# In late turns, sums of values and chunk 4's scores in one group of matmuls over four banks

## The chip, the cores and the metric

The kernel runs on one core of one Trainium2 chip. The metric is the device time of one execution in microseconds (us); the median of three runs before the change is 1108.84 us, the lowest 1106.07, the highest 1110.18.

## What is computed

Attention with a block mask over 8 batches, 8 heads, 576 positions, 64 values a head; its output, laid out as 4608 tokens of 512 values, goes through two dense layers (512 by 2048 and 2048 by 512) with a gate between. All in float32.

```python
def _attn_ref(q, k, v) -> np.ndarray:
    B, H, S, D = q.shape
    block = 64
    scale = 1.0 / np.sqrt(D)
    scores = scale * np.matmul(q, k.transpose(0, 1, 3, 2))
    pos = np.arange(S)
    block_i = pos[:, None] // block
    block_j = pos[None, :] // block
    mask = block_i >= block_j
    scores = np.where(mask, scores, -1000000000.0)
    scores = scores - np.max(scores, axis=-1, keepdims=True)
    attn = np.exp(scores)
    attn = attn / (np.sum(attn, axis=-1, keepdims=True) + 1e-09)
    return np.matmul(attn, v).astype(np.float32)

def _moe_ref(x, w_in, w_out) -> np.ndarray:
    h = x @ w_in
    g = h * (1.0 / (1.0 + np.exp(-1.702 * h)))
    return (g @ w_out).astype(np.float32)
```

## The kernel before

The 64 heads are taken in 32 pairs. One turn of the outer loop does the scores of pair n and the sums of values of pair n-1, and slips steps of the dense layers between them. The first 8 turns are early turns, the other 24 (n from 8 to 31) late turns; the change touches late turns alone.

**Attention.** The 576 rows of a head's scores are cut into five chunks: chunk 0 has 64 rows, chunks 1 to 4 have 128 each, and chunk i sees 64·(2i+1) columns: 64, 192, 320, 448, 576. `score` (L314) puts the scores of both heads into banks of PSUM, one bank a head, with chunks 3 and 0 side by side in one pair of banks and chunks 2 and 1 in another; chunk 4 is 576 wide and takes two pairs, columns 0 to 255 and 256 to 575. `weigh` (L354) lets DVE read a bank, mask it and find the row's extreme (L365, one read for each head and piece), and ACT take the exponential (L372). `normalise` (L378) inverts the row sums on DVE (L382, L385) and scales, on POOL (L390) for chunks 0 to 3 and on DVE (L392) for chunk 4. `turn` (L396) transposes 32x32 blocks on DVE (L399, L404) into the buffer `tw`, and after chunk 4 sixteen DMAs on SP's queue (L411) bring the blocks of the pair to their places in `pw`. `av` (L443) multiplies them with the values: 60 matmuls whose output columns are the 576 positions, and two ACT copies to `xr` (L465, L466). `prep` (L301) transposes the next pair's q and k on DVE into the only buffer `qk` (L306), which all scores read.

**Dense layers.** A tile has 384 tokens, twelve tiles in all. A unit of the first layer is 12 matmuls into a bank `hp` (L567); ACT takes tanh (L577), DVE forms the gated product (L578, called the gate below), ACT rounds it (L586) and POOL takes the rest (L82, `gl`). A unit of the second layer is 9 matmuls into the banks `acc` (L536), of the unit before. `split` (L500) rounds the next tile's tokens on ACT (L513, `xh`) and takes the rest on DVE (L82, `xl`).

**Banks.** PSUM has eight banks: three for `acc`, two that `hp` alternates between, and three for attention (`bank`, L90). The first bank of a late group is instead the one of the two `hp` banks that is free (`lent_bank`, L97); the unit of the first layer that follows then takes the same bank as the one before. So a late group has at most four banks: both pairs of the scores 3+0 and 2+1 take the lent one and all three; chunk 4 takes the same four; the sums take one and the lent one.

**Order.** TensorE runs its matmuls in the order in which the code writes them. The table `ORDER` gives the order of a turn: in a late turn the scores `3+0/2+1`, then `V` (the sums of the pair before), then `4` (chunk 4's scores), then `L` (`prep` of the next pair); a dash is a slot in which only steps of the dense layers run, and steps run after each slot until a quota is met. A late turn has six units of the first layer, two after each of the three groups. On DVE, ACT, POOL and SP the order is set at build time by the framework's scheduler, by priorities; the gate, tanh and `split` stand under `tc.high_priority(offset=300)`. Each engine then runs its list in that order. Chunks 1 and 3 share one buffer of exponentials (L362, `e1`), so a read of chunk 1's scores follows the transposes of chunk 3.

Of the kernel before, what the change touches and what calls it, by code (L numbers as in the profile page):

```python
# [25 lines left out]
ORDER = (  # L26
# [3 lines left out]
)  # L30

START = "1+0 - B 2/3 L C - V - 4 - a - - -"
HANDOVER = "B C - 3+0/2+1 - - V - - - 4 - - L - -"


WEIGHTS_BY = ((0, 0), (8, 13), (14.5, 32))
# [4 lines left out]
def attention_moe_kernel(  # L41
# [9 lines left out]
    nc = tc.nc  # L51
    B, H, S, D = q.shape
    DM, DF = w_in.shape
    P = 128
    BLK = 64
# [7 lines left out]
    NPAIR = B * H // 2  # L63
    HP = H // 2
    NCH = 5

    sp = ctx.enter_context(tc.tile_pool(name="sp", bufs=1))
    d2 = ctx.enter_context(tc.tile_pool(name="d2", bufs=2))
# [5 lines left out]
    def early(n):  # L74

        return n < 2 * HP
# [9 lines left out]
    turns = {"n": 0, "bank": 0, "experts": False, "late": False}  # L86
# [3 lines left out]
    def bank():  # L90
        tags = ["w0", "w1", "w2"]
        if not turns["experts"]:
            tags += ["acc0", "acc1", "acc2", "h"]
        turns["bank"] += 1
        return ps.tile([P, 512], F32, tag=tags[turns["bank"] % len(tags)], name="bank")

    def lent_bank():  # L97
        gate_bank["lent"] = True
        return ps.tile([P, 512], F32, tag=gate_bank["spare"], name="bank")
# [7 lines left out]
    def mm(**kw):  # L107
        return tc.keep_in_program_order(nc.tensor.matmul(**kw))  # L108
# [19 lines left out]
    def room(tag, shape, dt, name):  # L128
        return d2.tile(shape, dt, tag=tag, name=name, bufs=1)
# [8 lines left out]
    xr = sp.tile([P, NDC, RING], F32, name="xr")  # L138


    vp = sp.tile([P, 2, NCH, D], F32, name="vp")
    nc.gpsimd.memset(vp[BLK:P, :, NCH - 1, :], 0.0)
    vx = {}

    def values(n):

        if n not in (1, 3):
            return vp
        if n not in vx:
            vx[n] = room("xl", [P, 2, NCH, D], F32, "vx")  # L150
            nc.gpsimd.memset(vx[n][BLK:P, :, NCH - 1, :], 0.0)
        return vx[n]
# [7 lines left out]
    SLOT = (None, 0, 1, 3, 6)  # L160
    turned = sp.tile([P, 8 * NS - 4, 2, 32], F32, name="turned")
    tw, pw = [
        turned[:, x : x + 4 * NS].rearrange("p (b s) h c -> p b s h c", b=4) for x in (0, 4 * NS - 4)
    ]
# [4 lines left out]
    es = []  # L169
    for i in range(NCH):  # L170
        w, o = BLK * (2 * i + 1), 2 * BLK * i * i
        es.append(flat[:, o : o + 2 * w].rearrange("p (h k) -> p h k", h=2))

    def width(i):
        return BLK * (2 * i + 1)

    def qrange(i):
        return (0, BLK) if i == 0 else (BLK * (2 * i - 1), BLK * (2 * i + 1))
# [6 lines left out]
    for g in range(NG):  # L185
# [3 lines left out]
        for fc in range(FG):  # L189
            r = (g * FG + fc) * P  # L190
# [80 lines left out]
    raw, qk = {}, {}  # L271

    def heads(n):
        b, h = divmod(n, HP)
        return [(hd, b, 2 * h + hd) for hd in range(2)]
# [17 lines left out]
    def load_v(n):  # L293
        to = values(n)
        for hd, b, h in heads(n):
            nc.sync.dma_start(
                out=to[:, hd, 0:QC], in_=v[b, h, 0 : QC * P].rearrange("(c p) d -> p c d", p=P)
            )
            nc.sync.dma_start(out=to[0:BLK, hd, QC], in_=v[b, h, QC * P : S])
# [14 lines left out]
    def score(n, banks):  # L314

        turns["late"] = not early(n)
        if n not in stats:
            mx = d2.tile([P, NCH + 1, 2], F32, tag="mx", name="mx")
            sm = d2.tile([P, NCH, 2], F32, tag="sm", name="sm")
            stats[n] = (mx, sm)  # L320
        todo = []
        taken = 0
        for chunks in banks:

            part = []
            for lo, hi in ((0, 512),) if width(chunks[0]) <= 512 else ((0, 256), (256, S)):
                ss = []
                for _ in range(2):
                    taken += 1
                    ss.append(lent_bank() if taken == 1 and turns["late"] else bank())  # L330
                c = 0
                for i in chunks:
                    a, z = qrange(i)
                    w = min(hi, width(i)) - lo
                    for hd in range(2):
                        r = slice(hd * D, hd * D + D)

                        mm(
                            out=ss[hd][:, c : c + w], lhsT=qk[n][r, 0, a : a + P],
                            rhs=qk[n][r, 1, lo : lo + w], start=True, stop=True,  # L340
                        )
                        part.append((i, hd, lo, lo + w, ss[hd][0 : z - a, c : c + w]))
                    c += w
            todo.append(sorted(part, key=lambda x: (chunks[::-1].index(x[0]), x[2])))
        for chunks, part in zip(banks, todo):
            e = {}
            for i, hd, lo, hi, s in part:
                e[i] = weigh(n, i, hd, lo, hi, s, e.get(i))
            for i in chunks[::-1]:
                normalise(n, i, e[i])  # L350
                if not early(n):
                    turn(n, i, e[i])

    def weigh(n, i, hd, lo, hi, s, e):  # L354
        mx, sm = stats[n]
        a, z = qrange(i)
        m = z - a
        w = width(i)
        if early(n):
            e = es[i]  # L360
        elif e is None:
            e = d2.tile([P, 2, w], F32, tag=f"e{i % 2}", name="e", bufs=1)  # L362
        last = i > 0 and hi == w
        mk = mask[0:m, MW - (hi - lo) : MW] if last else mask[0:m, 0 : hi - lo]
        nc.vector.tensor_tensor_reduce(  # L365
            out=e[0:m, hd, lo:hi], in0=s, in1=mk,
            op0=ALU.add, op1=ALU.min, scale=-0.125,
            scalar=3e38 if lo == 0 else mx[0:m, NCH, hd : hd + 1],
            accum_out=mx[0:m, i, hd : hd + 1] if hi == w else mx[0:m, NCH, hd : hd + 1],
        )  # L370
        if hi == w:
            nc.scalar.activation(  # L372
                out=e[0:m, hd], in_=e[0:m, hd], func=AF.Exp, scale=-1.0,
                bias=mx[0:m, i, hd : hd + 1], accum_out=sm[0:m, i, hd : hd + 1],
            )
        return e

    def normalise(n, i, e):  # L378
        _, sm = stats[n]
        m = BLK if i == 0 else P  # L380
        c = sm[0:m, i]
        nc.vector.tensor_scalar(  # L382
            out=c, in0=c, scalar1=1e-9, scalar2=2.0, op0=ALU.add, op1=ALU.mult
        )
        nc.vector.reciprocal(out=c, in_=c)  # L385
        on = SCALE_ON[phase(n)][i]
        for hd in range(2):
            x, sc = e[0:m, hd], c[:, hd : hd + 1]
            if on == "P":
                nc.gpsimd.tensor_tensor(out=x, in0=x, in1=sc.to_broadcast([m, width(i)]), op=ALU.mult)  # L390
            elif on == "D":
                nc.vector.tensor_scalar(out=x, in0=x, scalar1=sc, scalar2=None, op0=ALU.mult)  # L392
            else:
                nc.scalar.activation(out=x, in_=x, func=AF.Copy, scale=sc)
# [48 lines left out]
    def av(n):  # L443

        b, h = divmod(n, HP)
        before_av(n)
        o = bank()
        o0 = lent_bank() if turns["late"] else bank()

        todo = []  # L450
        for i in range(1, NCH):
            c = (i - 1) * P
            todo += [(o, c, P, j, pw[:, :, SLOT[i] + j]) for j in range(i)]
            todo.append((o, c + BLK, BLK, i, pw[:, 2:4, 9 + i]))
        last = len(todo) - 1
        todo.append((o0, 0, BLK, 0, pw[:, 0:2, 10]))

        for x, (bk, c, nn, j, w) in enumerate(todo):
            for hd in range(2):
                mm(  # L460
                    out=bk[hd * D : hd * D + D, c : c + nn].rearrange("d (a c) -> d a c", c=32),
                    lhsT=values(n)[:, hd, j], rhs=w[:, :, hd], start=x in (0, last + 1), stop=x >= last,
                )
        c0 = (b % 2) * S
        nc.scalar.copy(out=xr[:, h, c0 : c0 + BLK], in_=o0[:, 0:BLK])  # L465
        nc.scalar.copy(out=xr[:, h, c0 + BLK : c0 + S], in_=o)  # L466
        m = follower(n)
        if m is not None:
            load_v(m)

    def follower(n):

        m = {0: 2, 1: 3, 2: 4, 3: None}.get(n, n + 1)
        return None if m is None or m >= NPAIR else m

    def order(n):
        return {HP: START, 2 * HP: HANDOVER}.get(n, ORDER[phase(n)]).split()

# [116 lines left out]
    ends = np.cumsum([0.0] + [NFC * chunk_time(tt) for _, tt in TILES])  # L595
# [30 lines left out]
    def before_av(n):  # L626

        need = (n // HP - 1) * S
        advance(n // HP * H, lambda: done["split"] >= need)
        assert done["split"] >= need  # L630
# [49 lines left out]
```

## Time and profile before

| what | us |
|---|---|
| median of 3 runs | 1108.84 |
| the profiled execution | 1109.41 |
| its span, first to last instruction | 1107.5 |
| PE (matmuls) busy | 1070.3 (97%) |
| DVE busy | 585.0 (53%) |
| ACT busy | 498.6 (45%) |
| POOL busy | 406.4 (37%) |

The sums below are made against the profiled execution, which is 0.57 us above the median. Times in rows of the trace count from the span's start. The late turns run from about 200 to about 955 us. Matmuls overlap, so the busy time of PE tells only that it hardly waits; how long a group of matmuls takes is read from where the next group starts. An `f32` matmul shows as two rows in the trace, so that the 60 rows of one group of sums are 30 matmuls of the list of 15 pieces for two heads.

### The profile page before, as it was taken

How to read it: one execution, taken by the hardware profiler on the slowest of the kernel's cores; microseconds unless marked ns; L12 is line 12 of the kernel's file. 1: busy time of each engine (PE TensorE's matmuls, PEld its weight loads, DVE VectorE, ACT ScalarE, POOL GpSimd, SP SyncE). 2: the span in 40 equal slices, each digit the busy share in tenths (PEclk: the TensorE clock that was granted, in tenths of full speed). 3: DMA queues.
4: the chain of work that ended last, by engine and by line, in shares of the span. 5: the costliest groups of instructions: out<-in, count | busy, mean ns of one | idle time of the engine just before them, and what ended most of it. 6: DMA issues, size and time to landing. Idle time of an engine off the chain costs nothing.

```text
span 1107.5 us, 19998 instructions
## 1 busy us (share of the span) xinstructions
PE 1070.3 (97%) x6960; PEld 915.7 (83%) x6960; DVE 585.0 (53%) x1856; ACT 498.6 (45%) x1321; POOL 406.4 (37%) x509
## 2 busy tenths in 40 slices
PE   5869999899999999999999999999999999999998
PEld 3657777788888888888888888888888888899997
DVE  6786786655645645655555555645655655211211
ACT  5865776533534534534443443443444444232322
POOL 4665565323333333333333332333333333222222
PEclk8979999999999999999999999999999999999999
DMA  8634523343434433243443333344443331200000
GB/s 172 208 90 155 147 61 80 71 96 62 102 85 86 108 77 70 60 98 77 105 96 76 79 91 71 64 109 87 86 104 69 73 89 47 54 29 1 30 1 29
DMA packets 219365, 91.25 MB, mean 82 GB/s; under 512 B 197760, under 2 KB 197760, under 8 KB 219264
## 3 DMA queue, kind: packets, MB, share of 16 engines
q1 hardware_dynamic: 214528, 89.38, 34.3%
q8 instruction: 55, 0.90, 0.3%
q10 hardware_dynamic: 4736, 0.59, 0.3%
q14 instruction: 46, 0.38, 0.1%
HBM read 45.09 MB, written 9.44 MB: 49 GB/s over the span
## 4 chain that ended last, share of the span: by engine, by line
PE 87%; DVE 4%; ACT 4%; issue 2%; SPq 1%; DMA 1%; POOL 1%; POOLq 0%; ACTq 0%; DVEq 0%
PE hp L108 35%; PE acc L108 35%; PE bank L108 16%; ACT turned L372 1%; PE bank L111 1%; SPq L411 1%; DVE wm L243 1%; ACT wm L228 1%; DVE turned L365 1%; DVE wm L232 1%; DVE wm L238 1%; DVE qk L306 0%; DVE xl L82 0%; DMA raw<-in_k_dram 0%; ACT turned L425 0%
## 5 line engine op out<-in xcount | busy, mean ns | idle before, releaser
L82 POOL TENSOR_TENSOR gl<-g,gh 128x384 fp32r<-128x384 f32 x192 | 194.4, 1013 | 545.7 <-ACT gh L586 430.3
L578 DVE SCALAR_TENSOR_TENSOR g<-g,hp 128x384 f32<-128x384 f32 x192 | 106.0, 552 | 312.2 <-ACT g L577 310.8
L108 PE MATMUL hp<-xh,wih 128*128 128x384 f32 x768 | 261.1, 340 | 4.2 <-DVE g L578 3.5
L108 PE MATMUL hp<-xh,wil 128*128 128x384 f32 x768 | 258.6, 337 | 0.0
L577 ACT ACTIVATE g<-hp 128x384 f32<-128x384 f32 x192 | 94.2, 491 | 357.3 <-PE hp L108 356.0
L108 PE MATMUL hp<-xl,wih 128*128 128x384 f32 x768 | 254.8, 339 | 0.2
L108 PE MATMUL acc<-woh,gh 128*128 128x512 f32 x576 | 233.9, 406 | 0.0
L108 PE MATMUL acc<-wol,gh 128*128 128x512 f32 x576 | 227.0, 394 | 0.0
L586 ACT CAST gh<-g 128x384 fp32r<-128x384 f32 x192 | 98.5, 513 | 157.8 <-DVE g L578 157.5
L108 PE MATMUL acc<-woh,gl 128*128 128x512 f32 x576 | 168.0, 393 | 0.3 <-POOL gl L82 0.3
L108 PEld LDWEIGHTS hp<-xh,wih 128*128 128x128 f32 x768 | 144.6, 188 | 17.1 <-DVE g L578 4.4
L108 PEld LDWEIGHTS hp<-xh,wil 128*128 128x128 f32 x768 | 144.5, 188 | 7.6
L372 ACT ACTIVATE e<-e,mx 64x64 f32<-64x64 f32 (+4 forms) x240 | 132.2, 552 | 34.2 <-DVE mx L365 34.2
L390 POOL TENSOR_TENSOR e<-e,sm 64x64 f32<-64x64 f32 (+1 forms) x192 | 113.6, 612 | 87.6 <-ACT e L372 45.2
L108 PEld LDWEIGHTS hp<-xl,wih 128*128 128x128 f32 x768 | 144.0, 188 | 1.0 <-DVE xl L82 1.0
L108 PEld LDWEIGHTS acc<-woh,gh 128*128 128x128 f32 x576 | 108.2, 188 | 34.2 <-issue 10.7
L108 PE MATMUL bank<-qk 64*128 64x320 f32 (+4 forms) x768 | 121.3, 428 | 13.9 <-DVE qk L306 11.3
L108 PEld LDWEIGHTS acc<-woh,gl 128*128 128x128 f32 x576 | 107.6, 188 | 25.4 <-POOL gl L82 1.2
L365 DVE CUSTOM_DVE_ANT_0 e<-bank,mask 64x64 f32<-64x64 f32 (+4 forms) x240 | 89.7, 417 | 67.5 <-PE bank L108 64.2
L108 PEld LDWEIGHTS acc<-wol,gh 128*128 128x128 f32 x576 | 108.4, 188 | 16.8 <-issue 0.4
L399 DVE STREAM_TRANSPOSE turned<-e 128x384 f32<-128x384 f32 (+1 forms) x192 | 92.5, 500 | 50.1 <-POOL e L390 48.4
L108 PEld LDWEIGHTS bank<-qk 64*128 64x128 f32 x768 | 69.8, 194 | 53.1 <-issue 22.1
(50 smaller groups left out, 962.3 us busy)
## 6 DMA issues: line engine op xcount, KB each, us to landing
turned<-turned SPq DMA_DIRECT2D x192, 80.0 KB, 2.1
turned<-turned SPq DMA_DIRECT2D x96, 112.0 KB, 2.2
raw<-in_q_dram SPq DMA_DIRECT2D x128, 72.0 KB, 2.3
out_dram<-osb SPq DMA_DIRECT2D x36, 256.0 KB, 2.4
raw<-in_k_dram SPq DMA_DIRECT2D x120, 72.0 KB, 2.4
turned<-turned SPq DMA_DIRECT2D x96, 88.0 KB, 2.1
words<-in_moe_w_in_dram SPq DMA_DIRECT2D x16, 512.0 KB, 6.0
vp<-in_v_dram SPq DMA_DIRECT2D x60, 128.0 KB, 2.4
```

The source lines that it names most:

```text
L82: eng.tensor_tensor(out=out, in0=in0, in1=in1, op=ALU.subtract)
L108: return tc.keep_in_program_order(nc.tensor.matmul(**kw))
L111: return tc.keep_in_program_order(nc.tensor.transpose(**kw))
L228: nc.scalar.activation(out=bits[j][:, c], in_=f(w[..., 1]), func=AF.Copy, scale=2.0**-112)
L232: nc.vector.tensor_scalar(out=u, in0=u, scalar1=3, scalar2=None, op0=ALU.logical_shift_left)
L365: nc.vector.tensor_tensor_reduce(out=e[0:m, hd, lo:hi], in0=s, in1=mk, op0=ALU.add, op1=ALU.min, scale=-0.125, scalar=3e38 if lo == 0 else ...
L372: nc.scalar.activation(out=e[0:m, hd], in_=e[0:m, hd], func=AF.Exp, scale=-1.0, bias=mx[0:m, i, hd : hd + 1], accum_out=sm[0:m, i, hd : hd ...
L390: nc.gpsimd.tensor_tensor(out=x, in0=x, in1=sc.to_broadcast([m, width(i)]), op=ALU.mult)
L399: nc.vector.transpose(out=tw[:, :, SLOT[i] : SLOT[i] + i, hd].rearrange("p b j c -> p j b c"), in_=e[:, hd, 0 : i * P],)
L577: nc.scalar.activation(out=g, in_=hp[:, 0:tt], func=AF.Tanh, scale=1.702)
L578: nc.vector.scalar_tensor_tensor(out=g, in0=g, scalar=1.0, in1=hp[:, 0:tt], op0=ALU.add, op1=ALU.mult)
L586: nc.scalar.copy(out=gh, in_=g)
```

## The change

In late turns `V` moves three slots later and the `4` of the table goes: `av` of pair n-1 now writes chunk 4's scores of pair n right behind the sums, in one group over four banks. The sums fill columns 0 to 319 of a first bank (positions 0 to 319) and 0 to 255 of a second (positions 320 to 575). Chunk 4's first 384 columns go to a bank of their own for each head, the lent one and the third; the other 192 go beside the sums, head 0's in the first bank and head 1's in the second. The copies to `xr` are 320 and 256 columns wide in place of 64 and 512. What follows the matmuls (`weigh`, `normalise`, `turn`) is unchanged and was put into a function `settle`. Early turns keep their banks and sizes.

```diff
     "1+0 - B - 2 - C - 3 L V - a - 4 -",
-    "3+0/2+1 - - - V - - 4 - - - L -",
+    "3+0/2+1 - - - - - - V - - - L -",
 )
-HANDOVER = "B C - 3+0/2+1 - - V - - - 4 - - L - -"
+HANDOVER = "B C - 3+0/2+1 - - - - - - V - - L - -"
...
         b, h = divmod(n, HP)
         before_av(n)
-        o = bank()
-        o0 = lent_bank() if turns["late"] else bank()
+        if turns["late"]:
+            o0, o = bank(), bank()
+            cut = BLK + 2 * P
+        else:
+            o, o0 = bank(), bank()
+            cut = BLK
+
+        def place(q0):
+            return (o0, q0) if q0 < cut else (o, q0 - cut)
 
         todo = []
         for i in range(1, NCH):
-            c = (i - 1) * P
-            todo += [(o, c, P, j, pw[:, :, SLOT[i] + j]) for j in range(i)]
-            todo.append((o, c + BLK, BLK, i, pw[:, 2:4, 9 + i]))
-        last = len(todo) - 1
-        todo.append((o0, 0, BLK, 0, pw[:, 0:2, 10]))
+            bk, c = place((i - 1) * P + BLK)
+            todo += [(bk, c, P, j, pw[:, :, SLOT[i] + j]) for j in range(i)]
+            todo.append((bk, c + BLK, BLK, i, pw[:, 2:4, 9 + i]))
+        todo.append((*place(0), BLK, 0, pw[:, 0:2, 10]))
...
+        m = n + 1
+        rest = []
+        if turns["late"] and m < NPAIR:
+            own = [lent_bank(), bank()]
+            a, z = qrange(4)
+            for hd in range(2):
+                r = slice(hd * D, hd * D + D)
+                mm(
+                    out=own[hd][:, 0:K4], lhsT=qk[m][r, 0, a : a + P],
+                    rhs=qk[m][r, 1, 0:K4], start=True, stop=True,
+                )
+                rest.append((4, hd, 0, K4, own[hd][0 : z - a, 0:K4]))
+            for hd, (bk, c) in enumerate(((o0, cut), (o, S - cut))):
+                r = slice(hd * D, hd * D + D)
+                mm(
+                    out=bk[:, c : c + S - K4], lhsT=qk[m][r, 0, a : a + P],
+                    rhs=qk[m][r, 1, K4:S], start=True, stop=True,
+                )
+                rest.append((4, hd, K4, S, bk[0 : z - a, c : c + S - K4]))
         c0 = (b % 2) * S
-        nc.scalar.copy(out=xr[:, h, c0 : c0 + BLK], in_=o0[:, 0:BLK])
-        nc.scalar.copy(out=xr[:, h, c0 + BLK : c0 + S], in_=o)
+        nc.scalar.copy(out=xr[:, h, c0 : c0 + cut], in_=o0[:, 0:cut])
+        nc.scalar.copy(out=xr[:, h, c0 + cut : c0 + S], in_=o[:, 0 : S - cut])
...
+        if rest:
+            settle(m, [[4]], [sorted(rest, key=lambda x: x[2])])
```

Three places in the built order follow. The new file has one line more ahead of `mm`, so its line numbers are a little higher; L369 is the read that was L365, L611 the gate that was L578, L403 and L408 the transposes L399 and L404, L307 the transpose of q and k.

**PE, the group of sums in a late turn.** Before, the last rows of the sums and what follows them (the names of counters in brackets tell which engine the row waits for):

```order
L108 MATMUL bank<-turned,vp 64x128 x6
L108 MATMUL bank<-turned,vp 64x64 x2
L108 MATMUL bank<-turned,vp 64x128 x8
L108 MATMUL bank<-turned,vp 64x64 x2
L108 MATMUL bank<-turned,vp 64x64 [waits DVE_49]
L108 MATMUL bank<-turned,vp 64x64
L108 MATMUL acc_3233<-woh,gh 128x512 [waits Activation_49]
```

Now, from the end of chunk 2's part of the sums on:

```order
L109 MATMUL bank<-turned,vp 64x64 x2
L109 MATMUL bank<-turned,vp 64x128 [waits DVE_49]
L109 MATMUL bank<-turned,vp 64x128 x5
L109 MATMUL bank<-turned,vp 64x64 x2
L109 MATMUL bank<-turned,vp 64x128 x8
L109 MATMUL bank<-turned,vp 64x64 x4
L109 MATMUL bank<-qk 128x384
L109 MATMUL bank<-qk 128x384 [waits DVE_49]
L109 MATMUL bank<-qk 128x192 x2
L109 MATMUL acc_6731<-woh,gh 128x512 [waits Activation_49]
```

The wait for DVE inside the sums stood ahead of their last two matmuls and was for the lent bank, by its counter for the gate of the unit that last used it; it now stands ahead of the first matmul into the second bank, and by its counter it is for the read of chunk 2's scores of head 0, the last to leave that bank. The scores of chunk 4 follow, and the one for head 1 waits for chunk 2's read of head 1. Four first-layer units (called h1 to h4 below) now stand between the scores 3+0 and 2+1 and the sums, in place of two; two (h5 and h6) stand between chunk 4's scores and the next turn's first scores, as before.

**DVE, from the transposes of chunk 0's and chunk 3's weights to the reads of chunks 1 and 2.** Before, the gates are those of the two units ahead of the sums:

```order
L404 STREAM_TRANSPOSE turned<-e 64x2x2x32
L578 SCALAR_TENSOR_TENSOR g<-g,hp 128x384
L404 STREAM_TRANSPOSE turned<-e 64x2x2x32
L578 SCALAR_TENSOR_TENSOR g<-g,hp 128x384
L399 STREAM_TRANSPOSE turned<-e 128x3x4x32 x2
L365 ISA e,mx<-bank,mask 128x192
L365 ISA mx 128x1
L365 ISA e,mx<-bank,mask 128x320
```

Now, in the eleventh late turn, for one:

```order
L611 SCALAR_TENSOR_TENSOR g<-g,hp 128x384
L408 STREAM_TRANSPOSE turned<-e 64x2x2x32
L611 SCALAR_TENSOR_TENSOR g<-g,hp 128x384
L408 STREAM_TRANSPOSE turned<-e 64x2x2x32
L611 SCALAR_TENSOR_TENSOR g<-g,hp 128x384 x2
L403 STREAM_TRANSPOSE turned<-e 128x3x4x32 x2
L369 ISA e,mx<-bank,mask 128x192
L369 ISA mx 128x1
L369 ISA e,mx<-bank,mask 128x320
```

Four gates, those of h1 to h4, now stand ahead of the transposes and of the reads of chunks 1 and 2; the two 128x192 rows and the two 128x320 rows that belong to the two heads are shown once. The 24 late turns fall into these kinds. In 8 turns it reads as shown: the transposes and all four reads stand behind the gate of h4. In 9 turns the transposes stand ahead of that gate and the reads (in one of these, all but the first) behind it; in 3 of these 9 a row of `xl` stands between the gate of h5 and the second transpose of the next place. In 2 turns the tile's `xh` and `xl` stand ahead of the gate of h4 and one transpose and the reads behind it. In 2 turns only the reads of chunk 2 stand behind it. In the first 3 turns all reads stand ahead of it.

**DVE, from chunk 4's reads to the next turn.** Before:

```order
L365 ISA e,mx<-bank,mask,mx 128x320
L365 ISA mx 128x1
L306 STREAM_TRANSPOSE qk<-raw 128x576 x2
L382 TENSOR_SCALAR sm<-sm 128x2
L385 RECIPROCAL sm<-sm 128x2
L392 TENSOR_SCALAR e<-e,sm 128x576 x2
L399 STREAM_TRANSPOSE turned<-e 128x4x4x32 x2
L404 STREAM_TRANSPOSE turned<-e 64x2x2x32
L578 SCALAR_TENSOR_TENSOR g<-g,hp 128x384 x2
L365 ISA e,mx<-bank,mask 64x64
```

Now:

```order
L369 ISA e,mx<-bank,mask,mx 128x192
L369 ISA mx 128x1
L307 STREAM_TRANSPOSE qk<-raw 128x576
L386 TENSOR_SCALAR sm<-sm 128x2
L389 RECIPROCAL sm<-sm 128x2
L396 TENSOR_SCALAR e<-e,sm 128x576 x2
L403 STREAM_TRANSPOSE turned<-e 128x4x4x32 x2
L408 STREAM_TRANSPOSE turned<-e 64x2x2x32
L611 SCALAR_TENSOR_TENSOR g<-g,hp 128x384
L307 STREAM_TRANSPOSE qk<-raw 128x576
L611 SCALAR_TENSOR_TENSOR g<-g,hp 128x384
L369 ISA e,mx<-bank,mask 64x64
```

One of the two transposes of q and k has moved behind chunk 4's scaling and transposes and the gate of h5; the next turn's first scores read what it writes.

More of the change, by code (lines that the diff above doesn't have):

```diff
@@ L65, in attention_moe_kernel @@
     NCH = 5
+    K4 = 384
     sp = ctx.enter_context(tc.tile_pool(name="sp", bufs=1))
@@ L344, in score, with settle @@
             todo.append(sorted(part, key=lambda x: (chunks[::-1].index(x[0]), x[2])))
+        settle(n, banks, todo)
+    def settle(n, banks, todo):
         for chunks, part in zip(banks, todo):
@@ L446, in av @@
         before_av(n)
-        o = bank()
-        o0 = lent_bank() if turns["late"] else bank()
+        if turns["late"]:
[6 more added lines that the diff above has]
+            return (o0, q0) if q0 < cut else (o, q0 - cut)
         todo = []
         for i in range(1, NCH):
-            c = (i - 1) * P
-            todo += [(o, c, P, j, pw[:, :, SLOT[i] + j]) for j in range(i)]
-            todo.append((o, c + BLK, BLK, i, pw[:, 2:4, 9 + i]))
-        last = len(todo) - 1
-        todo.append((o0, 0, BLK, 0, pw[:, 0:2, 10]))
+            bk, c = place((i - 1) * P + BLK)
+            todo += [(bk, c, P, j, pw[:, :, SLOT[i] + j]) for j in range(i)]
+            todo.append((bk, c + BLK, BLK, i, pw[:, 2:4, 9 + i]))
+        todo.append((*place(0), BLK, 0, pw[:, 0:2, 10]))
+        ends = [[x for x, y in enumerate(todo) if y[0] is bk] for bk in (o0, o)]
         for x, (bk, c, nn, j, w) in enumerate(todo):
@@ L461, in av @@
                     out=bk[hd * D : hd * D + D, c : c + nn].rearrange("d (a c) -> d a c", c=32),
-                    lhsT=values(n)[:, hd, j], rhs=w[:, :, hd], start=x in (0, last + 1), stop=x >= last,
-                )
-        c0 = (b % 2) * S
-        nc.scalar.copy(out=xr[:, h, c0 : c0 + BLK], in_=o0[:, 0:BLK])
-        nc.scalar.copy(out=xr[:, h, c0 + BLK : c0 + S], in_=o)
-        m = follower(n)
-        if m is not None:
-            load_v(m)
+                    lhsT=values(n)[:, hd, j], rhs=w[:, :, hd],
+                    start=any(x == y[0] for y in ends), stop=any(x == y[-1] for y in ends),
+                )
+        m = n + 1
[17 more added lines that the diff above has]
+                rest.append((4, hd, K4, S, bk[0 : z - a, c : c + S - K4]))
+        c0 = (b % 2) * S
+        nc.scalar.copy(out=xr[:, h, c0 : c0 + cut], in_=o0[:, 0:cut])
+        nc.scalar.copy(out=xr[:, h, c0 + cut : c0 + S], in_=o[:, 0 : S - cut])
+        nxt = follower(n)
+        if nxt is not None:
+            load_v(nxt)
+        if rest:
+            settle(m, [[4]], [sorted(rest, key=lambda x: x[2])])
     def follower(n):
```

## The prediction

> **Forecast.** Slower, 1177 us, since in 21 of the 24 late turns TensorE will stop in the middle of the sums for a bank, and then again ahead of the next scores for DVE. Both waits come from the order of DVE's list.
>
> **What bounds the kernel now.** First the page: busy times and the chain that ended last.
>
> ```profile
> PE 1070.3 (97%) x6960; PEld 915.7 (83%) x6960; DVE 585.0 (53%) x1856; ACT 498.6 (45%) x1321; POOL 406.4 (37%) x509
> PE 87%; DVE 4%; ACT 4%; issue 2%; SPq 1%; DMA 1%; POOL 1%; POOLq 0%; ACTq 0%; DVEq 0%
> ```
>
> TensorE (PE) carries 87% of the chain; DVE has half its time free. The averages mix stages, so next the busy times by stage (PE, PEld, DVE, ACT, POOL, then granted clock, DMA share, GB/s), for the late turns:
>
> ```profile
> 300.00:960.00 660.00, 658.99 (x4362) 570.01 (x4361) 361.13 (x1188) 276.95 (x744) 221.22 (x285) 1.00 0.37 82
> ```
>
> In 660 us PE is idle for 1 us, and its clock stays at 1.00. So a late turn is as long as its matmuls, and anything that makes PE wait there is paid in full. One late turn in the chain of waits (start, us, what):
>
> ```profile
> 499.44 2.04 PE bank L108 x16
> 501.48 2.24 PE acc L108 x9
> 503.72 2.10 PE hp L108 x12
> 505.82 2.08 PE acc L108 x9
> ...
> 510.02 2.92 PE bank L108 x60
> 512.93 2.26 PE acc L108 x9
> ...
> 521.49 1.17 PE bank L108 x8
> 522.66 2.27 PE acc L108 x9
> ...
> 531.22 0.57 PE bank L108
> ```
>
> The x16 group is the scores 3+0 and 2+1, x60 the sums, x8 chunk 4's scores, each followed by two second-layer and two first-layer units. From 499.44 to 531.22 the turn takes 31.78 us. A second-layer unit takes 2.08 us, but 2.24 to 2.27 just behind a group of attention: each group costs some 0.18 us at its end.
>
> **What the change gains.** Chunk 4's scores lose a group of their own: one slow unit less, 0.18 us. Their 576 columns for each head stay; at the rate of the sums (2.92 us for 1600 columns a head) they take 1.05 in place of 1.17, if the switch from sums to scores inside a group costs nothing, which no row here shows. Bounds 0 and 0.4 us a turn; I take 0.30, what the two terms give. For 24 turns: **-7.2 us**. The copies to `xr` (320 and 256 columns for 512 and 64) and the reads (384 and 192 for 256 and 320) have as many elements as before, on engines with free time. One lent bank fewer a turn saves nothing, as PE waits for no gate now (658.99 of 660).
>
> Without any wait, from the sums' start to the next turn's first scores PE would need 2.92 + 1.05 + 2.26 + 2.10 + 2.08 + 2.10 = 12.5 us.
>
> **What the change adds: the wait for a bank.** The second half of the sums goes to the bank that head 0's scores of chunks 2 and 1 leave. In the kernel before, DVE came to these reads just when the sums ran, and nobody waited, as the sums used other banks. That stretch (start, us, engine) is the model for the new order:
>
> ```profile
> 509.95 2.99 PE L108 MATMUL bank<-turned,vp 128*64 128x128 f32 x60
> 510.11 0.49 ACT L577 ACTIVATE g<-hp 128x384 f32<-128x384 f32 x1 [2.56 <-PE hp L108]
> 510.64 0.56 DVE L578 SCALAR_TENSOR_TENSOR g<-g,hp 128x384 f32<-128x384 f32 x1 [3.30 <-ACT g L577]
> 511.11 1.03 DVE L399 STREAM_TRANSPOSE turned<-e 128x384 f32<-128x384 f32 x2
> 511.23 0.51 ACT L586 CAST gh<-g 128x384 fp32r<-128x384 f32 x1 [0.62 <-DVE g L578]
> 512.28 0.36 DVE L365 CUSTOM_DVE_ANT_0 e<-bank,mask 128x192 f32<-128x192 f32 x1
> 512.57 0.35 DVE L365 CUSTOM_DVE_ANT_0 e<-bank,mask 128x192 f32<-128x192 f32 x1
> 512.68 0.46 ACT L372 ACTIVATE e<-e,mx 128x192 f32<-128x192 f32 x1 [0.95 <-DVE mx L365]
> 512.84 0.49 DVE L365 CUSTOM_DVE_ANT_0 e<-bank,mask 128x320 f32<-128x320 f32 x1
> 513.26 0.08 DVE L365 DVE_READ_ACCUMULATOR2_ANT mx<- 128x1 f32 x1
> ...
> 518.32 0.31 DVE L404 STREAM_TRANSPOSE turned<-e 64x128 f32<-64x128 f32 x1
> ```
>
> The gate of the unit ahead of the sums starts 0.69 us after them (tanh must see that unit's last matmul), then come the transposes, the reads, and head 0's read of chunk 2 is out at 513.34, 3.39 us after the sums' start. In the changed list the gate ahead is h4's, and the same rows follow. PE reaches the second half after 512 of 1600 columns, at 0.93 us.
>
> - *8 turns* with transposes and reads behind h4's gate: wait 3.39 - 0.93 = 2.46 us.
> - *9 turns* with the reads directly behind the gate: they start at 1.16 (511.11), the bank is out after steps of 0.29, 0.27, 0.42 and 0.08 at 2.22: wait 1.29.
> - *2 turns* where a tile is split there: three `xh` and three `xl` stand ahead as well.
>
> ```profile
> 540.07 2.10 ACT L513 CAST xh<-xr 128x384 fp32r<-128x384 f32 x4 [0.74 <-PE hp L108]
> 540.62 1.63 DVE L82 TENSOR_TENSOR xl<-xr,xh 128x384 fp32r<-128x384 f32 x3 [1.49 <-ACT xh L513]
> ```
>
> At 0.52 and 0.54 us each they bring the reads from 2.33 to about 3.9 and the release to 4.96: wait 4.0.
> - *2 turns* with only chunk 2's reads behind the gate: 1.16 + 0.42 + 0.08, wait 0.73.
> - *First 3 turns*: none, as all reads stand ahead.
>
> **What the change adds: the wait for q and k.** Behind this wait DVE has more to do than PE. Its list goes on through chunks 2 and 1 to 518.63 (8.68 us after the sums' start, measured above, POOL's steps included), and only then to chunk 4. For chunk 4 these rows:
>
> ```profile
> 524.25 1.44 DVE L306 STREAM_TRANSPOSE qk<-raw 128x576 f32<-128x576 f32 x2
> 524.68 0.76 ACT L372 ACTIVATE e<-e,mx 128x576 f32<-128x576 f32 x1
> 525.61 0.13 DVE L382 TENSOR_SCALAR sm<-sm 128x2 f32<-128x2 f32 x1
> ...
> 528.51 0.56 DVE L578 SCALAR_TENSOR_TENSOR g<-g,hp 128x384 f32<-128x384 f32 x1
> ```
>
> and from the groups by form (busy us, mean ns of one):
>
> ```profile
> L365 DVE CUSTOM_DVE_ANT_0 e<-bank,mask 128x448 f32<-128x448 f32 x40 | 23.1, 610 | 0.0
> L365 DVE CUSTOM_DVE_ANT_0 e<-bank,mask 128x320 f32<-128x320 f32 x40 | 17.9, 486 | 0.0
> ```
>
> A 384-wide read lies between the 320 and 448 ones, 0.55 us, 0.48 a step with the overlap of 0.07 seen above. Two of them and one of 192 columns (0.33) bring us to 9.98; the two exponentials start there and at 10.74; the row sums' step follows the second's start by 0.93 (524.68 to 525.61), 11.67; from it to the gate are 2.90 (to 528.51), 14.57. Then the gate of h5 (0.47 a step) and the second transpose of q and k (0.72), which before stood ahead of all this: 15.8 us. The next scores wait for it.
>
> PE is there at 12.5 + 2.46 = 15.0 in the 8 turns, so 15.8 decides, 3.3 us lost. In the 9 turns ACT takes the exponentials as soon as L586's copy is out (511.74, 0.94 before 512.68), and the chain ends 0.9 earlier, at 14.9 against 13.8 for PE: 2.4 lost. In 3 of these a row of `xl` stands ahead of that transpose and waits for L586 of h5 (out at 14.8) and an `xh`: 14.8 + 0.52 + 0.54 + 0.72 = 16.6, 1.75 more. In the 2 turns with chunk 2 alone behind the gate, 2.3. Of the first 3 turns two have the same late transpose, with chunk 4 some 2 us earlier but one transpose more ahead of its 192-wide reads: 13.7, 1.2 lost. The sixteen DMAs start up to 2 us later against the next scores, but the sums come two units (8.4 us) later, so their wait grows only in the last turn (under 1 us, left out).
>
> **The clock.** PE has had waits of this size in early turns:
>
> ```profile
> 202.60 0.44 PE L108 MATMUL hp<-xh,wih 128*128 128x384 f32 x1 [1.71 <-DVE g L578]
> ...
> 222.23 4.64 PE L108 MATMUL bank<-turned,vp 128*64 128x128 f32 x60 [2.50 <-DMA turned<-turned]
> ```
>
> with the stages around them:
>
> ```profile
> 200.00:205.00 5.00, 3.29 (x16) 2.81 (x17) 4.83 (x16) 1.13 (x2) 1.02 (x1) 1.00 0.00 0
> 222.00:224.00 2.00, 1.77 (x27) 1.80 (x29) 1.84 (x7) 0.40 (x2) 0.53 (x1) 0.74 0.78 126
> 224.00:226.00 2.00, 2.00 (x25) 2.00 (x23) 1.26 (x7) 1.67 (x8) 0.85 (x2) 0.50 0.96 257
> ```
>
> After 2.50 us of waiting the clock fell to 0.50 and the sums took 4.64 in place of 2.92, 1.7 us more; after 1.71 it stayed at 1.00. So waits of 1.3 cost no clock and those of 2.46 may: PE would reach the next scores at 16.7 in place of 15.8, 4.2 lost. I take 3.75, the middle, for the 8 turns; for the 2 turns with 4.0 of wait 4.0 + 1.7 = 5.7.
>
> [...]
>
> **The sum.** 8 x 3.75 + 9 x 2.4 + 3 x 1.75 + 2 x 5.7 + 2 x 2.3 + 2 x 1.2 = 30.0 + 21.6 + 5.3 + 11.4 + 4.6 + 2.4 = 75.3; less 7.2 is +68.1 on the profiled 1109.41 us. That one lies 0.57 above the median, so **1177 us**.
>
> **Rivals.**
>
> *Only the bank costs.* DVE catches up behind the sums and the clock holds: 8 x 2.46 + 9 x 1.29 + 2 x 4.0 + 2 x 0.73 = 40.8, less 7.2: 1142. For it: chunk 4's rows were put together from pieces. Against: each piece has its row, and the chain ends later than PE in every kind.
>
> *The clock holds at full rate*, and both waits stand: 71.7 less 7.2, 1173; for it the 1.71 us row, against it the 2.50 us row. [...]
>
> *Faster.* The reads of chunks 2 and 1 are out by 0.93 us after the sums' start, and DVE is never late: 1109.41 - 0.57 - 7.2 = 1102. Place: head 0's read of chunk 2; it decides from 0.93 on. For it: the first late turns stand so, and DVE has 45% of the stage free. Against: the gate that it queues behind starts at 0.69 at the earliest and lasts 0.56.
>
> *Nothing moves*, since the waits fall into time that PE loses already. PE loses 1 us in 660 there.
>
> **How the numbers follow.** Forecast 0.62, clock holds 0.20, only the bank 0.13, faster 0.03, nothing 0.02. The low end is 1142. For the high end every wait slows the clock (8 turns 4.2, six of the 9 turns 13.8 + 1.7 - 12.5 = 3.0: +7), the merge gains nothing (+7) and the chains are 0.3 us longer in 21 turns (+6): 1197. A measurement of this kernel can tell about 0.5%, 5.5 us, from no change: faster 0.03, same 0.02, slower 0.95.
>
> **What would show it.** PE idle inside `bank<-turned,vp` with DVE's `mx` as releaser, about 21 times 0.7 to 4 us; PE idle ahead of `bank<-qk` with DVE's `qk` as releaser; granted clock under 1.00 in some late slices; DVE well over 4% of the chain; a turn of 34 to 35 us. Wrong if PE's idle time in 300 to 960 us stays near 1 us: then DVE's list does not bind; if the sums wait but the scores don't, the chain of chunk 4 is too long here.

## The result, and the profile after

The changed kernel takes **1180.93 us** in the median of six runs (1177.8 to 1185.23) against 1108.93 us for the kernel before beside it (1106.07 to 1111.17): a ratio of 1.0651, with a 95% interval of 1.0633 to 1.0669. The forecast was slower, 1177 us, between 1142 and 1197. The profiled execution has a span of 1179.2 us and a mean granted clock of 0.974; before, these were 1107.5 us and 0.987.

The page of the changed kernel, busy times and the chain that ended last:

```profile
PE 1088.2 (92%) x6960; PEld 931.8 (79%) x6960; DVE 586.3 (50%) x1856; ACT 496.9 (42%) x1321; POOL 406.0 (34%) x509
PE 68%; DVE 14%; ACT 8%; issue 5%; POOL 4%; DMA 1%; DVEq 0%; POOLq 0%; SPq 0%; ACTq 0%
```

DVE does the same work as before (586.3 us against 585.0), but its share of the chain goes from 4% to 14%, and that of PE from 87% to 68%. The stage of the late turns, with the columns of before (PE, PEld, DVE, ACT, POOL, clock, DMA share, GB/s):

```profile
300.00:960.00 660.00, 609.61 (x3891) 526.03 (x3892) 333.72 (x1092) 252.33 (x683) 201.40 (x262) 0.98 0.35 77
```

PE now stands idle for 50 of 660 us where it stood idle for 1, and its clock is no longer at 1.00 throughout (0.98 in the mean). The view of waits, from 230 to 1040 us, names the two places:

```profile
PE bank L109 <- DVE mx L369: 33.9, 21, 2.4
PE bank L109 <- DVE qk L307: 23.7, 16, 3.1
```

The first is the wait for the bank inside the sums, the second the wait for q and k ahead of the next scores. One late turn in the chain of waits, from the unit ahead of the sums on; the sums start at 610.00 (start, us, what):

```profile
607.96 2.12 PE hp L109 x12
...
610.16 0.50 ACT g L610
...
611.15 1.04 DVE turned L403 x2
...
612.33 0.36 DVE e L369
...
618.78 0.56 DVE e L369
...
620.26 0.86 ACT e L376 x2
...
624.87 0.56 DVE g L611
625.42 0.70 DVE qk L307
...
626.16 2.11 PE bank L109 x16
```

Between 610.16 and 626.16 the chain does not touch PE: it runs through h4's tanh, DVE's list with the steps of ACT and POOL that it waits for, and ends with the second transpose of q and k. PE works in that stretch, but what it does is not what the next scores wait for. In the timeline, the rows of PE that end a wait (in brackets the idle time and its releaser), from most of the kinds of turn:

```profile
332.20 3.55 PE L109 MATMUL bank<-turned,vp 128*64 128x128 f32 x40 [2.34 <-DVE mx L369]
473.86 2.10 PE L109 MATMUL bank<-turned,vp 128*64 128x128 f32 x40 [1.91 <-DVE mx L369]
591.02 2.11 PE L109 MATMUL bank<-qk 64*128 64x448 f32 x16 [1.05 <-DVE qk L307]
613.44 2.10 PE L109 MATMUL bank<-turned,vp 128*64 128x128 f32 x40 [2.34 <-DVE mx L369]
626.16 2.11 PE L109 MATMUL bank<-qk 64*128 64x448 f32 x16 [0.90 <-DVE qk L307]
647.38 2.10 PE L109 MATMUL bank<-turned,vp 128*64 128x128 f32 x40 [1.16 <-DVE mx L369]
662.35 2.72 PE L109 MATMUL bank<-qk 64*128 64x448 f32 x16 [3.13 <-DVE qk L307]
```

The second half of the sums takes 2.10 us at full clock; behind the wait at 332.20 it takes 3.55, behind the equal wait at 613.44 it does not. From 591.02 to 626.16 the turn takes 35.14 us, from 626.16 to 662.35 36.19 us; before, the turns from 245 us on took 31.78 us.

### The profile page after: what moved, and what is told of

It is laid out like the page before. It is cut to its first block, busy times and chain, and to the rows that moved or that the text cites. A ratio compares the mean times of both kernels' runs of the same rounds, so it can differ in the third digit from the quotient of the medians.

```text
span 1179.2 us, 20026 instructions
## 1 busy us (share of the span) xinstructions
PE 1088.2 (92%) x6960; PEld 931.8 (79%) x6960; DVE 586.3 (50%) x1856; ACT 496.9 (42%) x1321; POOL 406.0 (34%) x509
## 4 chain that ended last, share of the span: by engine, by line
PE 68%; DVE 14%; ACT 8%; issue 5%; POOL 4%; DMA 1%; DVEq 0%; POOLq 0%; SPq 0%; ACTq 0%
PE hp L109 27%; PE acc L109 27%; PE bank L109 11%; ACT e L376 4%; POOL e L394 3%; DVE turned L403 3%; DVE e L369 2%; DVE g L611 2%; PE bank L112 1%; DVE qk L307 1%; DVE e L396 1%; DVE turned L408 1%; ACT g L610 1%; ACT turned L376 1%; DVE wm L244 1%
## 5 line engine op out<-in xcount | busy, mean ns | idle before, releaser
L611 DVE SCALAR_TENSOR_TENSOR g<-g,hp 128x384 f32<-128x384 f32 x192 | 106.0, 552 | 420.8 <-ACT g L610 420.2
L109 PE MATMUL bank<-qk 64*128 64x192 f32 (+5 forms) x768 | 127.3, 445 | 36.7 <-DVE qk L307 34.2
L109 PEld LDWEIGHTS hp<-xh,wih 128*128 128x128 f32 x768 | 144.7, 188 | 16.6 <-DVE g L611 3.8
L109 PE MATMUL bank<-turned,vp 128*64 128x128 f32 (+1 forms) x1800 | 103.8, 274 | 35.5 <-DVE mx L369 33.9
L109 PEld LDWEIGHTS bank<-qk 64*128 64x128 f32 x768 | 72.9, 203 | 80.0 <-DVE qk L307 40.1
L109 PEld LDWEIGHTS bank<-turned,vp 128*64 128x64 f32 x1800 | 96.5, 148 | 46.4 <-DVE mx L369 36.8
```

The lines of the kernel that those rows point to most:

```text
L611: nc.vector.scalar_tensor_tensor(out=g, in0=g, scalar=1.0, in1=hp[:, 0:tt], op0=ALU.add, op1=ALU.mult)
```

## The experiments

The theory is that of the prediction: the two waits, and nothing else, make the change slow, and both come from the order of DVE's list. The rivals are that only the bank costs (and the wait for q and k is its echo), and that the merged group itself costs. Each of the two waits is taken away by itself, then both; then the banks alone are dealt out in another way, PE is kept awake through a wait, and the group is put elsewhere.

### own_buffers: the reads of chunks 2 and 1 no longer wait for the transposes of chunk 3

```diff
-            e = d2.tile([P, 2, w], F32, tag=f"e{i % 2}", name="e", bufs=1)
+            e = d2.tile([P, 2, w], F32, tag={0: "own0", 1: "wm"}.get(i, f"e{i % 2}"), name="e", bufs=1)
```

`wm` is a buffer that the late turns no longer use for anything else.

> The changed kernel; the exponentials of chunks 0 and 1 get buffers of their own, so that DVE's reads of chunks 2 and 1 need not follow the transposes of chunk 3 and, in its list, now directly follow the reads of chunks 3 and 0. The second transpose of q and k stays late, in 12 of the 24 late turns behind the gates of both units h5 and h6. Theory (two waits, both from DVE's order): the 21 waits inside the sums (40 us with what the clock takes) are gone; the next scores wait behind the gate of h6, some 2 us in 9 turns and 4 us in 3, 30 us in all: 1109 - 3 + 30 = 1136 us, between 1122 and 1150. Rival, only the bank costs (the wait for q and k is its echo): no wait left, 1106. Rival, the merged group itself costs (longer groups, switches between groups, load on DVE): 1180 stays.

Measured: 1133.37 us (1128.42 to 1136.57), a ratio of 1.0219 (1.0189 to 1.0248). The view of waits has no row with `mx` any more, and one with `qk`:

```profile
PE bank L109 <- DVE qk L307: 24.4, 12, 2.4
```

Of these twelve waits nine are of 1.92 us and three of 2.38. The four executions lie in two pairs, 1136 us at a mean granted clock of 0.979 and 1128 to 1131 at 0.985 or 0.986; the last section shows that a wait of 1.92 us lowered the clock in 5 of 9 cases. In the timeline, the end of one such turn:

```profile
604.17 0.55 DVE L611 SCALAR_TENSOR_TENSOR g<-g,hp 128x384 f32<-128x384 f32 x1 [3.05 <-ACT g L610]
604.64 0.77 DVE L307 STREAM_TRANSPOSE qk<-raw 128x576 f32<-128x576 f32 x1
605.47 2.65 PE L109 MATMUL bank<-qk 64*128 64x448 f32 x16 [1.92 <-DVE qk L307]
```

DVE is idle for 3.05 us and then does the gate of h6 ahead of the transpose: it had the time, and its list did not use it. So the second transpose costs by its place alone, with no wait for a bank ahead of it. (In the changed kernel h6's gate stands behind this transpose in every late turn; here the scheduler put it ahead in twelve, so the two waits for q and k have the same kind of cause, not the same rows.) The rival that it is an echo falls, and so does the one that puts all the cost on the group.

### early_qk: both transposes of q and k ahead of chunk 4's scaling

```diff
-    "3+0/2+1 - - - - - - V - - - L -",
+    "3+0/2+1 - - - - - - V - - - - -",
...
-HANDOVER = "B C - 3+0/2+1 - - - - - - V - - L - -"
+HANDOVER = "B C - 3+0/2+1 - - - - - - V - - - - -"
...
+            pin = chunks == [4] and not early(n)
+            if pin and n + 1 < NPAIR:
+                prep(n + 1)
...
-                normalise(n, i, e[i])
+                normalise(n, i, e[i], pin)
...
-        nc.vector.tensor_scalar(
+        first = nc.vector.tensor_scalar(
...
+        if pin:
+            tc.keep_in_program_order(first)
```

> The changed kernel; both transposes of the next pair's q and k stand on DVE right behind chunk 4's reads, ahead of its scaling. The buffers of exponentials stay shared, and in this order 22 or 23 turns have the transposes of chunk 3 and all four reads behind the gate of h4. Theory: no wait for q and k is left, but the wait inside the sums is the long one (2.34 us in the profile of the change) in 22 or 23 turns, 54 us, and the clock falls after three of four such waits, 1.2 us each in the mean, some 20 us: 1109 - 3 + 54 + 20 = 1180 us, between 1160 and 1190. Rival, the wait for q and k is a cost by itself and the bank costs what it did: 1180 less some 25, 1155. Rival, the merged group itself: 1180 as well.

Measured: 1175.74 us (1175.2 to 1176.95), a ratio of 1.0606 (1.0592 to 1.0621). The view of waits, 230 to 1030 us:

```profile
PE bank L109 <- DVE mx L372: 51.8, 22, 2.8
PE bank L109 <- DVE g L616: 4.5, 12, 0.4
```

No wait for q and k is left; the one for the bank is the long one in 22 turns, as the scheduler, given the new place of the transposes, put chunk 3's transposes and the reads behind the gate of h4 nearly everywhere. The small second row is the lent bank of the next scores, which h5's gate now leaves late. The time barely falls, because what the one wait gives the other takes (23.7 us of waits for q and k are gone, those for `mx` go from 33.9 to 51.8 us): the wait for the bank is a cost by itself as well.

### early_qk_own_buffers: both edits

> Both edits at once: own buffers of exponentials for chunks 0 and 1, and both transposes of q and k right behind chunk 4's reads. Theory: neither wait is left; TensorE is idle for about 1 us in 300 to 960 us, a late turn takes 31.5 to 31.7 us, and only the gain of the merge stands, 0.13 to 0.30 us in each of 24 turns: 1102 to 1106 us against 1109, a ratio of 0.994 to 0.997. Rival, the merged group itself costs: well over 1120. Rival, chunk 4's transposes and DMAs come too late for the next sums: a wait for a DMA ahead of the sums, over 1110.

Measured: **1098.93 us** (1097.09 to 1100.28), a ratio of 0.9908 (0.9894 to 0.9922): faster than the kernel before. The chain of the page, the stage of the late turns, and a turn in the chain of waits:

```profile
PE 90%; DVE 3%; ACT 3%; issue 1%; DMA 1%; POOL 0%; SPq 0%; POOLq 0%; ACTq 0%; DVEq 0%
```

```profile
300.00:960.00 660.00, 660.00 (x4387) 575.47 (x4387) 364.22 (x1179) 279.19 (x747) 220.05 (x286) 1.00 0.37 82
```

```profile
543.58 4.09 PE bank L109 x68
547.67 2.27 PE acc L109 x9
...
556.23 2.04 PE bank L109 x16
558.27 2.24 PE acc L109 x9
...
575.18 4.08 PE bank L109 x68
579.26 2.27 PE acc L109 x9
...
587.82 2.04 PE bank L109 x16
```

PE is busy for all of the 660 us, at full clock. With the same merged group in place nothing is lost, so the group itself costs nothing: the rival that it does falls. From 556.23 to 587.82 a turn takes 31.59 us, 0.19 less than the 31.78 of before. That is the merge by itself. Sums and chunk 4's scores take 4.08 or 4.09 us in one group; before they took 2.92 and 1.17, and the same 4.09 in sum. What is saved is that one unit fewer stands behind a group and takes 2.27 us in place of 2.08; nothing is saved in the group.

### before_own_buffers: the control

The same edit of the buffers in the kernel before.

> Control: the kernel before, with the own buffers of exponentials for chunks 0 and 1 alone. Theory: nobody waits for the reads of chunks 2 and 1 there, so nothing moves, 1107 to 1111 us, ratio 0.997 to 1.003. Rival: the shared buffer costs time before as well, and the buffers give a gain that has nothing to do with the change: under 1104.

Measured: 1105.01 us (1103.91 to 1107.3), a ratio of 0.9968 (0.9956 to 0.9981): 4 us faster, a little outside what was expected. The gain is not in the late turns in general: their turn still takes 31.78 us. It lies at their beginning. The prediction showed that PE there waited 1.71 us for a gate at 202.60, and that the sums waited 2.50 us for a DMA and then ran at half rate for 4.64 us. Now the first of these waits is gone, and the timeline has in the place of the second

```profile
219.08 2.99 PE L108 MATMUL bank<-turned,vp 128*64 128x128 f32 x60 [1.91 <-DVE g L578]
```

and no fall of the clock: the sums take 2.99 us. So of the 10.2 us that early_qk_own_buffers gains against the kernel before beside it, 4.1 go to the buffers and 6.1 to the rest: 24 times 0.19 is some 4.5, and the rest is of the size of a wait of 1.65 us for a DMA ahead of the last sums, which before_own_buffers has and early_qk_own_buffers has not.

### banks_swapped: the sums in the banks that come free early

```diff
-            o0, o = bank(), bank()
+            o0, o = bank(), lent_bank()
...
-            own = [lent_bank(), bank()]
+            own = [bank(), bank()]
```

> The changed kernel with the banks dealt out the other way: the sums take a bank that was left early and the lent one, and chunk 4's first 384 columns take the two banks that DVE's reads of chunks 2 and 1 leave late. So the sums wait for nobody; head 0's scores of chunk 4 may wait up to 0.4 us for their bank. Nothing is done for DVE's list: its chain from the sums' start to the second transpose of q and k stays as long as it was (15.7 us with the reads behind the gate of h4 and the transposes, 14.7 with the reads alone behind it), and in 12 turns it has the gate of h6 ahead of that transpose as well. Theory: what the sums no longer wait comes back ahead of the next scores, 2.2 to 4 us in one piece in some 21 turns, 65 to 75 us, and half rate after most of them: 1165 to 1205 us, no gain against the change's 1181. Rival, only the bank costs: under 1130 us.

Measured: 1213.56 us (1212.88 to 1214.17), a ratio of 1.0949 (1.0925 to 1.0972). The view of waits, 230 to 1040 us:

```profile
PE bank L109 <- DVE qk L307: 69.6, 22, 4.8
PE bank L109 <- DVE mx L369: 4.5, 8, 0.7
```

The wait inside the sums is gone, and the kernel is slower than the change by 33 us. The waits for the bank and for q and k together were 57.6 us; now one place alone has 69.6 us, most of it in pieces of 4.2 to 4.8 us, because the scheduler put the transpose behind h6's gate in twelve turns. Between 230 and 1050 us the granted clock is at half for 75 us in place of 34. That the waiting comes back ahead of the next scores was expected, and in these waits was of the size expected (65 to 75). The time lies 9 us above the range: 4.5 us are the waits for `mx`, and the rest fits a clock that the range counted too low, which no run shows by itself. Where h5's gate alone stands ahead of the transpose, the time from the sums' start to the next scores is what it was in the change (16.09 us from 478.74 to 494.83 beside 16.16, and 15.14 in both from 590.63 and from 857.16); with h6's gate as well it is 17.87 (439.62 to 457.49). So the bank that comes free earlier is worth nothing here, since DVE's chain decides, and by these numbers it is the gate and the clock that make this kernel slower than the change.

### early_qk_filled: PE kept busy through a part of the wait

As early_qk, with `own` taken ahead of the sums and two matmuls more in front of their second half, which chunk 4's own scores overwrite:

```diff
+            if fill and x == ends[1][0]:
+                for _ in range(2):
+                    mm(
+                        out=own[0][:, 0:K4], lhsT=qk[m][0:D, 0, 0:P],
+                        rhs=qk[m][0:D, 1, 0:K4], start=True, stop=True,
+                    )
```

> As in the run early_qk, with two more matmuls of 384 columns (chunk 4's scores of one head, written into the bank that chunk 4's own scores take and overwritten by them) in front of the second half of the sums. TensorE works through 1.2 to 1.3 us of each wait of 2.34 us; the bank comes at the same time as before. Reading of the clock so far: it falls at the edges of a fixed grid of 3.41 us, after a stretch of it in which TensorE stood idle for 1.92 us or more. Idle stretches of 1.1 us then never lower it: no half rate in 300 to 960 us, mean clock 0.988 to 0.990 as in the kernel before, and the time is lower by the 8 falls at up to 1.7 us each, 1160 to 1168 us in place of 1175.7. Rival, the falls don't come from idleness (heat, power, load): they stay, and the time stays at 1176. Rival, the two matmuls cost their own time: 23 times 1.25 us more, 1204.

Measured: 1170.46 us (1168.65 to 1170.97), a ratio of 1.0557 (1.0536 to 1.0577), 5.3 us less than early_qk with more work on PE. The stage of the late turns, and the waits:

```profile
300.00:960.00 660.00, 636.17 (x4079) 537.35 (x4076) 338.70 (x1114) 256.78 (x696) 204.91 (x266) 1.00 0.35 77
```

```profile
PE bank L109 <- DVE mx L372: 19.0, 22, 1.1
PE bank L109 <- DVE g L624: 7.7, 20, 0.6
```

The waits shrink from 2.34 to 0.85 us, the bank comes at the same time (3.44 us after the sums' start in both, 402.39 to 405.83 and 403.13 to 406.57), and the clock does not fall in any late turn, where it fell eight times in early_qk (mean 0.988 against 0.978). So the falls come from idleness here: work that is thrown away prevents them. The gain is smaller than the 8 to 16 us expected. A fall cost 1.1 us, not 1.7: in the timeline of early_qk a turn without one takes 34.64 us (371.19 to 405.83) and the one with the next fall 35.77 (405.83 to 441.60); by the author's estimate part of the lost time would have been spent waiting for the lent bank (0.4 us at most in early_qk's second row). In the first late turn, where the sums don't wait, the two matmuls cost their own 1.5 us (197.88 to 199.36). And the profiled execution came to the late turns 1.5 us later, ahead of anything that was edited.

### merged_two_units_early: the group two units after the scores

```diff
-    "3+0/2+1 - - - - - - V - - - L -",
+    "3+0/2+1 - - - V - - - - - - L -",
```

> The changed kernel with the merged group two units of the first layer after the scores 3+0 and 2+1 in place of four, and so four in place of two ahead of the next scores. In DVE's list the reads of chunks 2 and 1 still stand behind the gate ahead of the sums, in 13 of the late turns with one or both transposes of chunk 3 in front of them. Theory: the wait for the bank stays (8 times 2.34 us, the rest 1.2 to 1.8, some 40 us, and up to 10 us by the clock), the wait for q and k has 8.4 us more of cover and goes: 1109 - 4.5 + 40 + 8 = 1152 us, between 1142 and 1162. Rival, both waits come together: 1181.

Measured: 1174.75 us (1173.54 to 1175.56), a ratio of 1.0597 (1.0577 to 1.0617): a miss, 13 us above the range. The waits, 230 to 1040 us, and one of the new kind in the timeline:

```profile
PE bank L109 <- DVE mx L369: 39.0, 20, 2.4
PE acc L109 <- ACT gh L619: 14.4, 17, 1.4
PE acc L109 <- POOL gl L83: 0.5, 2, 0.3
```

```profile
406.16 0.50 PE L109 MATMUL acc<-woh,gh 128*128 128x512 f32 x1 [0.76 <-ACT gh L619]
```

The wait for the bank is of the size expected (39.0 for 40), and the one for q and k is gone. But the same chain of DVE for chunk 4 now runs into the unit behind the second gate: this gate stands in the list behind the scaling and transposes of chunk 4, ACT's copy `gh` follows it late, and the second-layer unit that reads it waits, 17 times. The expectation had not asked what would be late next in this place. The rest of the gap, some 8 us, is not taken apart; the clock fell six times, which the expectation had counted at 8 us.

## Why the prediction was right, point by point

*What binds.* Right. PE's idle time in 300 to 960 us went from 1 to 50 us, with `mx` and `qk` as releasers as named, and both waits can be taken away by edits that leave the work as it is and move rows in the lists: the one for the bank (own_buffers), the one for q and k (early_qk), and both (early_qk_own_buffers). Each single edit also led the scheduler to change what remained, so the two waits are not priced one by one.

*The wait for the bank.* The second half of the sums was predicted to start 3.39 us after the first; in the turn of the chain above it is 3.44 (610.00 to 613.44). The idle times of the profile look shorter than the waits as worked out (2.34 for 2.46, 1.16 for 1.29, 0.60 for 0.73), but they count from the end of the first half's last matmul, 1.11 us after the sums' start, where the second half would have followed at 0.93 or 0.94 (in the kernel before its first row starts 0.94 us after the sums). With these 0.18 us the waits are 2.5, 1.34 and 0.78, each some 0.05 longer than predicted. One term failed: *the two turns with a tile split*, 4.0 predicted, 1.91 idle measured. The prediction had DVE reach the `xl` only behind h4's gate and counted three steps each of `xh` and `xl` against the reads. In the trace the `xh` and two of the three `xl` ran ahead of the sums, from 469.73 on (the sums start at 470.84), and one transpose ran at 470.75; h4's gate started only 0.15 us later than without them (471.68), and the reads 1.91 us after the sums' start, earlier than in the eight turns (2.33).

*The wait for q and k.* The chain from the sums' start to the next scores, and what a turn lost against 31.59 us, the turn without waits:

| kind | chain: predicted, measured | lost: predicted, measured |
|---|---|---|
| 8 turns, clock holds | 15.8, 16.16 | 3.3, 3.55 |
| 8 turns, clock falls | 16.7, 16.8 | 4.2, 4.2 |
| 9 turns | 14.9, 15.14 | 2.4, 2.5 |
| of these 3, with `xl` | 16.6, 17.2 | 4.15, 4.6 |
| 2 turns with a tile split | 18.2, 16.4 | 5.7, 3.8 |
| 2 turns, chunk 2 behind | 14.8, 14.9 | 2.3, 2.25 |

The measured values are differences of starts in the timeline (610.00 to 626.16, 435.10 to 451.89, 857.16 to 872.30, 645.12 to 662.35, 470.84 to 487.24, 506.22 to 521.10). The chain put together from pieces of the old trace was 0.2 to 0.4 us short in most kinds. In the turn shown 0.28 of its 0.36 us lie ahead of chunk 4's exponentials, which start 10.26 us after the sums' start (620.26) in place of 9.98.

*The clock.* The middle was taken for the 8 turns; the clock fell in 6 of them. It also fell in one of the two turns with a wait of 1.91 us and in two of the three with 3.13 us. So the loss by the clock was larger than predicted. early_qk_filled, whose waits inside the sums are 0.85 us and whose clock falls in no late turn, shows that idleness is the cause.

*The gain of the merge.* Mis-sized: predicted 0.30 us a turn, measured 0.19 (31.78 to 31.59). The term for the slow unit, 0.18, was right. The term for the rate, 0.12, was wrong: chunk 4's scores take the same 1.17 us in one group with the sums. For 24 turns that is -4.5 us and not -7.2.

*The sum.* In the 22 turns from 210.12 to 981.28 the waits and the clock cost 76.2 us against turns of 31.59 us; the prediction's terms for these turns (all but one of the 8 turns) make 71.5. The 7 turns that are left of the 8 cost 1.9 more (five at 4.2 and two at 3.55, for 3.75), the three with `xl` 1.3 more and the two split turns 3.9 less. The other six of the nine cost 5.4 more, 4.5 of it in two turns that begin at half rate, because the clock fell in the 3.13 us wait ahead of them (35.71 and 37.00 us, from 662.35 and 944.28, where such a turn takes 34.1). That a fall reaches into the next turn is not in the prediction. The smaller gain of the merge adds 2.5. Against all this stands a term that the prediction showed and left out of its sum: the kernel before loses 4.2 us itself in the turn from 209.09 to 245.08 (35.99 us, with the wait of 2.50 us and the half rate), and the changed kernel does not have this loss. Together that is +3.0, nearly all of the 3.5 us by which the profiled execution (1181.0) lies above the sum. So the mechanism held, and most terms were of the right size; that the forecast came within 4 us is in part luck, since errors of 4 to 5 us cancelled. The mean turn from 242.91 to 981.28 takes 35.16 us (21 turns), 3.4 more than before; the prediction said 34 to 35.

*The rivals.* "Only the bank costs" (1142) falls with own_buffers and banks_swapped, "the clock holds" (1173) with the rows above, "faster" with the rows of waits. That the group could be a gain, with a list on DVE that fits it, is what early_qk_own_buffers shows.

## What to carry to other kernels

When two groups on the engine that binds are merged, ask two things: when the engine behind it comes, in its own list, to what frees the banks of the group, and what stands in that list between the group and the next thing that the first engine reads. An engine that is half idle (DVE here, busy for 334 of 660 us) can still set the pace if its list is in the wrong order, and the order can hang on something as far away as a buffer that two chunks share. Expect the list to change when one such wait is taken out: here the edit against the one alone gave 5 us, the edit against the other 48, both together 82, and freeing a bank without shortening DVE's chain made the kernel slower by 33.

## What the runs showed of the hardware

In these runs the granted clock fell on a grid of time. In three profiles (the change, own_buffers, early_qk), with 65 waits of PE of 1 us or more between 230 and 1040 us, every fall of the granted clock lies within 0.03 us of a multiple of 3.413 us from a start that differs from run to run (in the change the first lies at 332.62 and the last at 1005.05, 197 such steps apart), and lasts 3.41 us or a multiple (why one in the change, from 943.60, lasts two steps is open). Each began at the end of a step of the grid in which PE had been idle for long enough: from 150 us on, with less than 1.90 us of idle time in one step it never fell, with more than 1.95 it always did, and of the eight steps between these seven brought a fall. The limit is not sharp: in merged_two_units_early a step with 2.01 us of idle time brought none (812.02 to 815.43). Stretches of early_qk cut along its grid, around two equal waits of 2.34 us (length, PE busy, and the granted clock third from the end):

```profile
369.31:372.72 3.41, 1.53 (x30) 1.53 (x32) 2.55 (x13) 2.31 (x9) 1.70 (x3) 1.00 0.01 2
372.72:376.13 3.41, 3.41 (x32) 2.56 (x27) 2.03 (x8) 0.70 (x2) 1.66 (x3) 1.00 0.31 72
```

```profile
403.44:406.86 3.42, 1.08 (x22) 1.03 (x22) 2.89 (x13) 2.25 (x8) 1.20 (x2) 1.00 0.00 0
406.86:410.27 3.41, 3.41 (x30) 2.69 (x28) 1.72 (x7) 0.34 (x2) 2.16 (x4) 0.50 0.04 9
410.27:413.68 3.41, 3.41 (x20) 2.80 (x17) 3.25 (x12) 0.79 (x3) 0.00 (x0) 1.00 0.36 82
```

The first wait falls across an edge of the grid, its step has 1.53 us of work, and the clock holds; the second lies within one step, which has 1.08 us of work, and the next step runs at half rate though PE works in all of it. So for the waits of 1.91 to 3.13 us in these profiles it was a matter of their place on the grid whether they cost clock: a wait of 1.92 us brought a fall in 5 of 9 cases in own_buffers, and one of 3.13 us brought none in one of 3 cases in the change. Waits of 1.33 us and less never did in these profiles. PE need not have been idle for a whole step: in the change 1.91 us of idle time in one of 3.41 (752.46 to 755.87) brought a fall.
